# Loading transformed data four steps ahead, and copying turned weight pieces with the scalar engine

## The chip, the cores and the metric

The kernel runs on one core of one Trainium2 chip. The metric is the device time of one execution in microseconds (us); lower is better. TensorE is written PE, its weight loads PEld, VectorE DVE, ScalarE ACT, GpSimd POOL. SyncE (SP) computes nothing here: it issues nearly all transfers, in the order of the program, and where a transfer has to wait for a buffer or for data, SP stands still and everything behind it waits too.

## The reference, cut to what matters

```python
X = np.fft.rfft(x, axis=1)                      # x: 8 batches x 3072 x 256
Yr = Xr @ w_r - Xi @ w_i + b_r                  # mixing, complex, 256 x 256
Yi = Xr @ w_i + Xi @ w_r + b_i
Y  = shrink(Yr) + 1j * shrink(Yi)               # towards zero by 0.01
y  = np.fft.irfft(Y, n=3072, axis=1)            # 24576 tokens x 256
h  = y @ w_in;  g = h - tanh(h);  x2 = g @ w_out          # d_ff = 2048
logits = x2 @ phi                               # 32 slots
# soft mixture of 8 experts: softmax over tokens in, softmax over slots out
```

All is float32 at the interface.

## The kernel before

The kernel has three parts: a spectral phase (the transform, the mixing and the way back, to about 700 us), a token phase (the gate and the logits, chunk by chunk) and a short expert phase. The change touches the spectral phase alone.

**The spectral phase** does a real transform of length 3072 as 96 x 32. For each batch, `f1_half` multiplies by the 96-point table and stores the result to DRAM (`ad`), in 8 pieces. `load_a2` reads it back in another order: one transfer of 512 KB holds the data of two *pairs* of frequency groups. `f2_pair` does the 32-point transform of one pair. `split_sum`, `mix_part`, `add_bias` and `shrink` do the mixing, `i1_pair` the first stage of the way back, `i2_half` the second.

The loop at L576 runs over steps `s`: step `s` does `f2_pair` of pair `i` of batch `b`, with `b, i = divmod(s, 12)`, so there are 96 steps of some 6 to 9 us, and in the same step the mixing of pair `s-1`, `i1_pair` of pair `s-2`, the way back of an earlier batch, and the first stage of a later batch (`piece`). An even step issues `load_a2` for step `s + 2`. Its tiles come from the pool `fa2`, which has three buffers. Nothing is scheduled by the compiler here: each engine runs the instructions in the order in which the program writes them.

**The pieces of weights.** `w_out` and `w_in` come as 64-bit floats, in 32 pieces, four for each batch of 12 steps. In a step `s` that has a piece, `load_w` loads it into the one buffer `raw`; `narrow`, one step later, queues 11 DVE instructions that make float32 values out of it, which `pump` hands out over two steps (L505, L508). `use_w` at `s+4` turns the piece on PE into the PSUM tile `pt` (L453) and DVE copies `pt` to `wt` (L455). `fold_w` at `s+5` multiplies it (`pw`); for the 16 pieces of `w_out` DVE writes the negative to `wp` (L488), for the 16 of `w_in` DVE adds it up in `mw` (L478, L480).

**The bank.** `pf2` of `f2_pair`, `pt` and `pw` share one PSUM tag, `f2`, with a single buffer. So `f2_pair` of a step can start only when its data `a` has landed and when the last `pt` or `pw` of the step before has been read out.

On SP the order within a step is: stores of the step before (`flush`), loads of `x`, loads `v2`, stores and loads of the weight pieces, stores of `y`, `load_a2`, and last `load_w`.

Of the kernel before, what the change touches and what calls it, by code (L numbers as in the profile page):

```python
# [12 lines left out]
AF = mybir.ActivationFunctionType  # L13
ALU = mybir.AluOpType
# [110 lines left out]
def spectral_phase(tc, nb, x, w_r, w_i, b_r, b_i, tb, yd, w_in, w_out, phi, ident, wo32, md, wh, wl, wp, wy, ew):  # L125

    nc = tc.nc
    with ExitStack() as late, ExitStack() as mid, ExitStack() as ctx:
# [32 lines left out]
        NP = NG // 2  # L161
# [20 lines left out]
        def load_f2(g0, g1):  # L182
            nc.sync.dma_start(out=f2[:, 128 * g0:128 * g1], in_=tb["f2"][:, 128 * g0:128 * g1])
# [16 lines left out]
        def load_mix():  # L200
            for w in (w_r, w_i):
                t = thp.tile([128, 512], F32, tag="sw", name="wst", bufs=3)
                nc.sync.dma_start(
                    out=t.rearrange("p (h e) -> p h e", h=2), in_=w.rearrange("(h p) e -> p h e", p=128)
                )
                tables.append(t)
# [10 lines left out]
        def load_tables():  # L217
            nc.sync.dma_start(out=i1, in_=tb["i1"])
            nc.sync.dma_start(out=bias[:, 0:256], in_=b_r.partition_broadcast(128))
            nc.sync.dma_start(out=bias[:, 256:512], in_=b_i.partition_broadcast(128))  # L220
            nc.gpsimd.memset(dh.bitcast(F32), 0.0)
            nc.gpsimd.memset(dl_.bitcast(F32), 0.0)
# [214 lines left out]
        def use_w(j):  # L437
            src, r, q = pieces[j]
            t = wnew.pop(j)
            if src is w_in:  # L440
                n = slice(256 * (q % 2), 256 * (q % 2) + 256)
                if wl[r][q // 2] is None:
                    wl[r][q // 2] = ew.wp.tile([128, 512], F32R, tag=f"wl{r}{q // 2}", name="wl")
                h = wh[r][q // 2][:, n]
                nc.scalar.activation(h, t, AF.Copy)
                nc.gpsimd.tensor_tensor(
                    out=wl[r][q // 2][:, n], in0=t, in1=h.bitcast(F32), op=ALU.subtract
                )
            else:
                nc.sync.dma_start(out=wo32[128 * r:128 * r + 128], in_=t)  # L450
            pt = ps.tile([128, 2, 128], F32, tag="f2", name="pt", bufs=1)
            for k in range(2):
                nc.tensor.transpose(pt[:, k, :], t[:, 128 * k:128 * k + 128], ident)  # L453
            wt = dcp.tile([128, 2, 128], F32, tag="wt", name="wt")
            nc.vector.tensor_copy(wt, pt)  # L455
            wtr[j] = wt

        def load_wf(j):
# [7 lines left out]
        def fold_w(j):  # L466

            src, r, q = pieces[j]
            wt = wtr.pop(j)
            if src is w_in:  # L470
                pw = ps.tile([128, 288], F32, tag="f2", name="pw", bufs=1)
                wf = wfs.pop(j)
                for k in range(2):
                    F = 2 * q + k
                    nc.tensor.matmul(pw[:, 0:256], wt[:, k, :], wf[:, k], start=k == 0, stop=k == 1, skip_group_check=True)
                    nc.tensor.matmul(pw[:, 256:288], wt[:, k, :], wp[:, F, :], start=False, stop=k == 1, skip_group_check=True)
                if q == 0:
                    nc.vector.tensor_scalar(out=mw, in0=pw, scalar1=-1.0, scalar2=None, op0=ALU.mult)  # L478
                else:
                    nc.vector.tensor_tensor(out=mw, in0=mw, in1=pw, op=ALU.subtract)  # L480
                if q == 7:
                    nc.sync.dma_start(out=md[128 * r:128 * r + 128], in_=mw[:, 0:256])
                    nc.vector.tensor_copy(wy[:, r], mw[:, 256:288])
                return
            pw = ps.tile([128, 32], F32, tag="f2", name="pw", bufs=1)
            for k in range(2):
                nc.tensor.matmul(pw, wt[:, k, :], ph[:, k, :], start=k == 0, stop=k == 1)
            nc.vector.tensor_scalar(out=wp[:, r, :], in0=pw, scalar1=-1.0, scalar2=None, op0=ALU.mult)  # L488

        chores = []  # L490

# [34 lines left out]
        if True:  # L526
            load_f2(0, 2)
            for i in range(8):
                for j in range(2):
                    f1_half(0, i, j)  # L530
                if i == 2:
                    load_mix()
            split_mix()
            load_a2(0, 0)
            load_f2(2, 8)
            load_tables()
            load_f2(8, 16)
            load_f2(16, NG)
            load_late_tables()
            T = nb * NP  # L540

            pieces_at = {}
            for k in range(1, nb):
                for j in range(8):
                    pieces_at[NP * (k - 1) + j + (2 if k == 1 else 0)] = (k, j)

            def piece(t):
                return [pieces_at[t]] if t in pieces_at else []

            for t in range(3):  # L550
                for j in piece(t):
                    load_x(*j)

            i2_at, v2_at, y_steps = {}, {}, {}
            for k in range(nb):
                t = NP * k + NP
                if k < nb - 2:
                    steps = [t + 4 + j for j in range(4)] + [t + 8 + j // 2 for j in range(8)] + [t + 12 + j for j in range(4)]
                    gap = 1
                else:  # L560
                    steps = [t + 4 + j // 2 for j in range(16)]
                    gap = 1
                for j in range(8):
                    for u in range(2):
                        i2_at.setdefault(steps[2 * j + u], []).append((k, j, u))
                    v2_at.setdefault(max(t + 3, steps[2 * j] - 3), []).append((k, j))
                for h in range(2):
                    for u in range(3):
                        t1 = steps[8 * h + 7] + 1 + gap * u
                        y_steps.setdefault(t1 if k < nb - 1 else T + NP - 1, []).append((k, h, 2 * u))  # L570

            slots = [NP * k + j for k in range(nb) for j in range(1, 9, 2)]
            due_w = {}
            for j in range(len(pieces)):
                due_w.setdefault(slots[len(slots) * j // len(pieces)], []).append(j)
            for s in range(T + NP):  # L576
                b, i = divmod(s, NP)
                flush()
                if s < T:
                    f2_pair(b, i)  # L580
                pump(1)
                for j in due_w.get(s - 1, ()):
                    narrow(j)
                for j in piece(s + 3):
                    load_x(*j)
                m = divmod(s - 1, NP) if 1 <= s <= T else None
                if m:
                    mix_part(*m, 0)
                    add_bias(*m)
                for j in v2_at.get(s, ()):  # L590
                    load_v2(*j)
                for j in piece(s):
                    f1_half(*j, 0)
                due = i2_at.get(s, ())
                for j in due[:(len(due) + 1) // 2]:
                    i2_half(*j)
                for j in due_w.get(s - 5, ()):
                    fold_w(j)
                for j in due_w.get(s - 4, ()):
                    use_w(j)  # L600
                for j in due_w.get(s - 3, ()):
                    load_wf(j)
                if s < T:
                    split_sum(b, i)
                pump(3)
                if m:
                    mix_part(*m, 1)
                if m:
                    mix_part(*m, 2)
                for j in piece(s):  # L610
                    f1_half(*j, 1)
                if m:
                    shrink(*m)
                pump(2)
                for j in due[(len(due) + 1) // 2:]:
                    i2_half(*j)
                if 2 <= s <= T + 1:
                    i1_pair(*divmod(s - 2, NP))
                for j in y_steps.get(s, ()):
                    store_y(*j)  # L620
                if 4 <= s < 12:
                    load_i2(s - 4)
                if s + 2 < T:
                    load_a2(*divmod(s + 2, NP))
                for j in due_w.get(s, ()):
                    load_w(j)
                if s == T:
                    ctx.close()
                if s == T + 3:
                    mid.close()  # L630
                yield
# [865 lines left out]
```

## Time and profile before

| | |
|---|---|
| time, median of 3 runs | 2306.78 us (2300.38 to 2307.19) |
| time of the profiled execution | 2304.85 us |
| its span, first to last instruction | 2302.7 us |
| mean granted clock of PE | 0.989 |
| PE busy | 2224.2 us, 97% of the span |
| DVE busy | 1761.4 us, 76% |
| ACT busy | 1449.5 us, 63% |
| POOL busy | 656.4 us, 29% |
| transfers, share of the 16 DMA engines on SP's queue | 76.7% |

An engine's row says how long it had an instruction in work. PE is in work nearly all the time, so the time is PE's work plus what PE stands still, plus what it loses where the granted clock is 0.5 instead of 1.0 (1.2 in place of 2.4 GHz).

### The profile page before, as it was taken

What the parts mean: (1) busy time and instruction counts of PE and PEld (TensorE: products, weight loads), DVE (VectorE), ACT (ScalarE), POOL (GpSimd) and SP (SyncE); (2) the same over time, 40 slices, a digit from 0 to 9 for tenths busy, and PEclk for the clock granted to TensorE, in tenths of its full rate; (3) what the DMA queues carried; (4) which work ended last, traced back from release to release, by engine and by line L of the source; (5) the groups of instructions that cost most, each with busy time, mean ns of one, the idle gap of its engine ahead of it and who ended that gap; (6) DMA issues with size and microseconds to landing.
All of it is one profiled execution on the core that took longest, in us unless ns stands there. A gap on an engine that the chain in (4) does not pass through costs nothing.

```text
span 2302.7 us, 51129 instructions
## 1 busy us (share of the span) xinstructions
PE 2224.2 (97%) x19832; PEld 1823.4 (79%) x19832; DVE 1761.4 (76%) x3605; ACT 1449.5 (63%) x2347; POOL 656.4 (29%) x666
## 2 busy tenths in 40 slices
PE   6899999999989999999999999999999999999989
PEld 4677777878878888888888888888887888888757
DVE  4888787888885877778777877777877787777634
ACT  2455565556545777667667676767767677666624
POOL 1333333434432422222222222222222222222111
PEclk8999999999999999999999999999999999999999
DMA  8678888888666777777777777777777777777899
GB/s 231 215 210 255 245 248 240 248 251 250 206 212 193 169 179 186 177 171 174 168 176 178 176 180 184 182 175 175 172 169 175 175 180 179 186 174 175 238 342 366
DMA packets 404018, 471.16 MB, mean 205 GB/s; under 512 B 36160, under 2 KB 351808, under 8 KB 403392
## 3 DMA queue, kind: packets, MB, share of 16 engines
q1 hardware_dynamic: 403664, 467.85, 76.7%
q8 instruction: 157, 2.57, 0.5%
q14 instruction: 85, 0.70, 0.1%
q10 hardware_dynamic: 112, 0.04, 0.0%
HBM read 164.45 MB, written 106.17 MB: 118 GB/s over the span
## 4 chain that ended last, share of the span: by engine, by line
PE 56%; DMA 6%; SPq 3%; ACT 1%; issue 0%; DVE 0%; ACTq 0%
PE ph L771 35%; PE pd L1020 7%; PE pl L892 6%; DMA yr<-yd 4%; PE p_out L1319 3%; SPq L860 3%; PE pd L812 2%; DMA ewt<-in_moe_w 2%; PE pl L828 1%; PE pl L900 1%; ACT g L782 0%; DMA gq<-in_moe_w 0%; SPq L1006 0%; DVE gt L846 0%; SPq L1308 0%
## 5 line engine op out<-in xcount | busy, mean ns | idle before, releaser
L782 ACT ACTIVATE g<-ph 128x512 f32<-128x512 f32 x752 | 448.4, 596 | 378.2 <-PE ph L771 353.4
L789 DVE TENSOR_TENSOR g<-ph,g 128x512 f32<-128x512 f32 x564 | 373.3, 676 | 157.1 <-PE ph L771 146.8
L846 DVE STREAM_TRANSPOSE gt<-g 128x512 f32<-128x512 f32 x752 | 476.1, 681 | 12.9 <-DMA gq<-gt 7.8
L771 PE MATMUL ph<-th,s 128*128 128x256 f32 x2256 | 482.0, 286 | 2.1 <-ACT g L782 2.1
L771 PEld LDWEIGHTS ph<-th,s 128*128 128x128 f32 x2256 | 377.8, 189 | 41.4 <-issue 19.4
L793 ACT ACTIVATE g<-g 128x1024 f32<-128x1024 f32 x376 | 392.6, 1054 | 1.5
L771 PE MATMUL ph<-tl,s 128*128 128x256 f32 x1128 | 318.3, 282 | 0.0
L771 PE MATMUL ph<-y,wh 128*128 128x256 f32 x1128 | 316.4, 280 | 0.0
L771 PE MATMUL ph<-yh,wl 128*128 128x256 f32 x1128 | 315.7, 280 | 0.0
L771 PE MATMUL ph<-yh,wh 128*128 128x256 f32 x1128 | 315.6, 280 | 0.0
L684 POOL TENSOR_TENSOR tl<-tr,th 128x512 fp32r<-128x512 f32 x94 | 122.1, 1300 | 383.1 <-ACT th L683 349.6
L678 POOL TENSOR_TENSOR tr<-y 128x256 f32<-128x256 f32 x92 | 68.1, 740 | 553.8 <-DMA y<-yd 553.8
L372 POOL TENSOR_TENSOR sw<-t,c 64x256 f32<-64x256 f32 x192 | 169.5, 883 | 182.2 <-DVE c L364 155.2
L771 PEld LDWEIGHTS ph<-tl,s 128*128 128x128 f32 x1128 | 213.8, 190 | 0.0
L771 PEld LDWEIGHTS ph<-yh,wh 128*128 128x128 f32 x1128 | 212.9, 189 | 0.1
L771 PEld LDWEIGHTS ph<-yh,wl 128*128 128x128 f32 x1128 | 212.4, 188 | 0.0
L771 PEld LDWEIGHTS ph<-y,wh 128*128 128x128 f32 x1128 | 212.2, 188 | 0.1
L892 PE MATMUL pl<-g,wp 128*32 128x256 f32 x3072 | 196.8, 386 | 0.0
L1020 PE MATMUL pd<-gq,et 128*32 128x512 f32 x1504 | 181.6, 593 | 0.5 <-DMA gq<-gt 0.5
L281 PEld LDWEIGHTS pf<-f,a 128*128 128x128 f32 x768 | 102.1, 198 | 94.3 <-issue 34.0
L407 PEld LDWEIGHTS pi<-i,v 96*128 96x128 f32 x1024 | 130.2, 195 | 26.1 <-issue 19.9
L281 PE MATMUL pf<-f,a 128*128 128x128 f32 x768 | 108.0, 286 | 42.8 <-DMA a<-ad 22.0
(225 smaller groups left out, 4586.3 us busy)
## 6 DMA issues: line engine op xcount, KB each, us to landing
gq<-gt SPq DMA_DIRECT2D x1504, 128.0 KB, 3.1
xt<-in_x SPq DMA_DIRECT2D x64, 384.0 KB, 5.8
vd<-vs SPq DMA_DIRECT2D x96, 256.0 KB, 4.1
v<-vd SPq DMA_DIRECT2D x64, 384.0 KB, 6.5
yd<-yt SPq DMA_DIRECT2D x48, 512.0 KB, 5.9
y<-yd SPq DMA_DIRECT2D x48, 512.0 KB, 5.9
yr<-yd SPq DMA_DIRECT2D x48, 512.0 KB, 4.1
a<-ad SPq DMA_DIRECT2D x47, 512.0 KB, 6.5
```

The source lines that it names most:

```text
L281: nc.tensor.matmul(p[:, :, h, gg, :], t[:, gg, 128 * h:128 * h + 128], f2[:, 128 * g:128 * g + 128], start=True, stop=True,)
L372: eng.tensor_tensor(out=v[64 * ri:64 * ri + 64, gg], in0=t[q, e], in1=c[q, e], op=ALU.subtract)
L407: nc.tensor.matmul(p[:, a, :], t[:, 4 * u + a, :], i2[:, 96 * n2:96 * n2 + 128], start=True, stop=True)
L684: nc.gpsimd.tensor_tensor(out=lo, in0=t, in1=hi.bitcast(F32), op=ALU.subtract)
L771: nc.tensor.matmul(o[:, 256 * j:256 * j + 256], a[u][:, 128 * j:128 * j + 128], y[v], start=new and j == 0 and k == 0, stop=n in (2, 3, 4) ...
L782: nc.scalar.activation(e[n], o.rearrange("p (j n) -> p j n", j=2), AF.Copy)
L789: nc.vector.tensor_tensor(out=h, in0=o, in1=h, op=ALU.add)
L793: nc.scalar.activation(g, g, AF.Tanh)
L846: nc.vector.transpose(out=t[:, :, 2 * (p % 4) + u, :], in_=g[:, u, :].rearrange("p (c i) -> p c i", i=32))
L860: nc.sync.dma_start(out=o[32 * q:32 * q + 32], in_=t[32 * a:32 * a + 32, q])
L892: nc.tensor.matmul(lp[c][q:q + 32, 0:256], wp[:, 2 * p + f, :], half_of(gs[c, p + f // 2][:, f % 2], h), start=p == 0 and f < 2, stop=Fals ...
L1020: nc.tensor.matmul(o[32 * a:32 * a + 32, f], ex[c][:, k, :], g[a][:, k], start=k == 0, stop=k == 3)
```

## The change

Loads of `a` are issued two steps earlier, that is four steps ahead of their use. The second load of the first batch moves to the start, directly behind the second part of the table `f2`. The first pair of the second batch (t = 12) keeps its place two steps ahead, and t = 14 goes directly behind it. The first pairs of the batches after that (t = 24, 36, ..., 84) are loaded four steps ahead as well, which is the step whose `flush` issues the last store of that batch's `ad`. The three buffers stay. The copy of `pt` to `wt` and the negation of `pw` into `wp` go from DVE to ACT; `mw` stays on DVE.

```diff
@@ use_w
             wt = dcp.tile([128, 2, 128], F32, tag="wt", name="wt")
-            nc.vector.tensor_copy(wt, pt)
+            nc.scalar.activation(wt, pt, AF.Copy)
             wtr[j] = wt
@@ fold_w
-            nc.vector.tensor_scalar(out=wp[:, r, :], in0=pw, scalar1=-1.0, scalar2=None, op0=ALU.mult)
+            nc.scalar.activation(wp[:, r, :], pw, AF.Copy, scale=-1.0)
@@ before the loop
             load_a2(0, 0)
             load_f2(2, 8)
+            load_a2(0, 2)
             load_tables()
@@ end of step s
-                if s + 2 < T:
-                    load_a2(*divmod(s + 2, NP))
+
+                for t in (s + 2, s + 4):
+                    if 4 <= t < T and (t == NP) == (t == s + 2):
+                        load_a2(*divmod(t, NP))
                 for j in due_w.get(s, ()):
                     load_w(j)
```

(`load_a2` does nothing for odd pairs; `NP` is 12 and `T` is 96.)

## Rows read from the trace of the kernel before

**Rows 1.** Groups of instructions; busy us, mean ns, idle us before it with releasers.

```profile
L281 PE MATMUL pf<-f,a 128*128 128x128 f32 x768 | 108.0, 286 | 42.8 <-DMA a<-ad 22.0 <-DVE wt L455 9.0 <-DVE t L363 3.7
```

**Rows 2.** Busy time by stretch: PE, PEld, DVE, ACT, POOL, clock, DMA share, GB/s.

```profile
60.00:192.00 132.00, 121.91 (x752) 93.34 (x751) 117.02 (x248) 67.36 (x118) 49.41 (x60) 0.99 0.76 225
192.00:700.00 508.00, 486.17 (x3242) 404.08 (x3240) 429.45 (x876) 292.19 (x486) 195.98 (x233) 0.98 0.79 235
```

**Rows 3.** Timeline around step 46, SP: start us, duration us, instruction.

```profile
336.20 0.38 SPq L153 DMA_DIRECT2D ad<-asb  x1
...
338.20 1.02 SPq L269 DMA_DIRECT2D a<-ad  x1
```

**Rows 4.** Timeline of PE at the start of step 46.

```profile
347.40 1.17 PE L281 MATMUL pf<-f,a 128*128 128x128 f32 x8 [3.52 <-DVE c L364]
```

**Rows 5.** Tile a, 337 to 349 us: its transfers.

```profile
DMA to landing us min/median/max: 7.8/8.4/9.1
```

**Rows 6.** Waits of SP, 60 to 700 us: total us, times, longest.

```profile
SPq L431 <- DVE dl L508: 150.1, 24, 8.2
...
SPq L269 <- DMA ad<-asb: 1.0, 1, 1.0
```

**Rows 7.** Timeline of the first steps, all engines.

```profile
28.72 2.05 PE L281 MATMUL pf<-f,a 128*128 128x128 f32 x8 [6.90 <-DMA a<-ad]
...
33.27 0.57 SPq L269 DMA_DIRECT2D a<-ad  x1
...
34.75 0.35 SPq L431 DMA_DIRECT2D raw<-in_moe_w_out  x1
...
44.81 2.05 PE L281 MATMUL pf<-f,a 128*128 128x128 f32 x8 [6.66 <-DMA a<-ad]
...
49.99 0.28 DVE L505 TENSOR_SCALAR da<-raw 128x256 int32<-128x256 int32 x1
```

**Rows 8.** Tile raw, 34 to 36 us: its transfer.

```profile
DMA to landing us min/median/max: 12.7/12.7/12.7
```

**Rows 9.** Busy time by stretch, first steps; columns as in rows 2.

```profile
38.00:44.80 6.80, 0.14 (x2) 0.02 (x1) 2.38 (x4) 0.00 (x0) 1.75 (x2) 0.73 1.07 228
```

**Rows 10.** Waits of PE, 60 to 192 us.

```profile
PE pf L281 <- DVE wt L455: 6.4, 5, 1.6
PE pf L281 <- DMA a<-ad: 1.5, 2, 0.9
PE pf L281 <- DVE wp L488: 1.2, 1, 1.2
PE pi L379 <- POOL sw L372: 0.6, 1, 0.6
```

**Rows 11.** Waits of DVE, 50 to 192 us.

```profile
DVE da L505 <- DMA raw<-in_moe_w_out: 7.7, 6, 1.5
DVE xml L293 <- ACT xmh L292: 2.7, 3, 1.3
```

**Rows 12.** Groups of instructions by shape; columns as in rows 1.

```profile
L455 DVE COPY wt<-pt 128x256 f32<-128x256 f32 x32 | 13.2, 412 | 0.0
...
L920 ACT ACTIVATE le<-pl 64x256 f32<-64x256 f32 x47 | 17.3, 367 | 0.0
```

**Rows 13.** Line L488: duration ns min/median/max, first and last start us.

```profile
L488 DVE TENSOR_SCALAR wp<-pw x16: 179/181/193, 77.9 to 366.2; 128x32 f32<-128x32 f32 x16
```

**Rows 14.** Busy time by stretch, around three waits; columns as in rows 2.

```profile
263.00:270.00 7.00, 7.00 (x36) 7.00 (x35) 4.17 (x9) 2.27 (x4) 1.68 (x3) 0.51 0.65 237
...
348.00:352.00 4.00, 4.00 (x24) 4.00 (x23) 3.59 (x6) 1.63 (x3) 1.25 (x2) 0.57 1.03 361
...
652.00:659.00 7.00, 4.33 (x20) 4.36 (x21) 6.04 (x13) 2.66 (x5) 2.49 (x3) 0.51 0.46 142
```

**Rows 15.** Waits of ACT, 60 to 700 us.

```profile
ACT xmh L311 <- DVE xmf L304: 74.2, 49, 4.0
```

**Rows 16.** Page, part 6: issues, KB each, median us to landing.

```profile
ad<-asb SPq DMA_DIRECT2D x58, 384.0 KB, 4.0
```

## The prediction

> **What bounds the kernel now.** I read the page first: PE is in work for 97% of the span and the chain that ended last runs mostly through PE, so time is won only where PE stands still or runs at the low clock. Then I read the groups by shape for the line where the change acts. Before the first product of `f2_pair` PE stood idle for 42.8 us in all [rows 1]; that is the whole pool from which this change can draw directly. Then the busy time by stretch, for who stands behind PE: DVE is in work for 117.0 of 132 us from 60 to 192 us, and for 429.5 of 508 us from 192 to 700 [rows 2]. ACT has 292.2 of 508 there, so it has room.
>
> The names that the list of waits gives need a check, since `f2_pair` waits for two things at once: its data and the bank. Step 46 shows how. PE stood idle 3.52 us until 347.40, put down to DVE L364 [rows 4], which `f2_pair` does not need. SP issued the load for this step at 338.20 [rows 3], and the longer of the two transfers in that stretch took 9.1 us [rows 5]: it landed at 347.3, and PE started 0.1 us later. This was a wait for the load. Why was it issued so late? `load_w` waits for the single buffer `raw`, until DVE has done the last of the 11 instructions on the piece before: SP stood there 150.1 us in all, 24 times, up to 8.2 us [rows 6]. Everything behind `load_w` is held, also the next step's load of `a`, which is needed two steps later at most.
>
> So there are two independent causes, in part at the same steps: loads that come late because SP stands, and a bank that DVE empties late because it is behind with its queue. Taking one away alone would leave the other. The change takes both.
>
> **The change part by part.** I split the 42.8 us by time. *Start:* 6.90 us before the very first `f2_pair`, whose load is not moved, and 6.66 us for the second load [rows 7], which is. *60 to 192 us:* 6.4 + 1.5 + 1.2 = 9.1 us [rows 10]. *After 192 us:* the rest, 42.8 - 6.9 - 6.7 - 9.1 = 20.1 us, of which I count 19, leaving 1 for waits of other kinds.
>
> *Start.* The second load was issued at 33.27 and PE waited for it until 44.81 [rows 7]. From 38 to 44.8 us the DMA engines were full, share 1.07 at 228 GB/s [rows 9]. Placed behind `f2[2:8]` it goes ahead of the other tables and the first pieces of `x`, so it should be there when PE asks at 38.1; the 6.66 us vanish for PE. But the load of t = 4 now takes its old place, which is ahead of the first `raw`. That transfer was issued at 34.75 and took 12.7 us [rows 8], so it landed at 47.4. With 512 KB more ahead of it at 228 GB/s it lands 2.2 us later, an estimate of 49.7. DVE first touched `raw` at 49.99 [rows 7], and `shrink` stands behind that in DVE's queue. So DVE gets on only 0.3 us earlier (2.5 us if `raw` isn't delayed), while PE gets on 6.7 us earlier and then waits for `shrink`.
>
> *60 to 192 us.* Here PE cannot pass DVE. DVE's idle time from 50 to 192 us is mostly 7.7 us of waiting for `raw` and 2.7 us of waiting for ACT's `xmh` [rows 11]; the first is made by its own queue (end of one piece, load, first instruction of the next) and stays. And PE already waited for the output of `shrink` at `i1_pair` [rows 10], so a wait removed from `f2_pair` reappears there. What the stretch gains is what DVE gains: 0.3 us from the start, eight copies `wt` at 0.41 us [rows 12] = 3.3 us, of the eight `wp` at 0.18 us [rows 13] those two that are not just ahead of a wait for `raw` = 0.4 us, and the 2.7 us in which DVE waited for work. That is 6.7 us at most, of 15.8 us that vanish at `f2_pair`. I take 5.5.
>
> *After 192 us.* Here DVE has time to catch up in every batch: it is idle for 78.5 of 508 us [rows 2], and only four of twelve steps' pieces overload it. So a wait that vanishes is mostly won. Also DVE loses 0.41 us of work in every second step with pieces. I take 16 of the 19 us; the other 3 go where DVE, now behind a faster PE, brings the sums or `shrink` too late.
>
> *Clock.* Three times after 192 us the granted clock stood at 0.51 to 0.57 for 4 to 7 us [rows 14], each time behind one of the longest waits at `f2_pair`. PE was in work for 7.0, 4.0 and 4.33 us of these. At the full level, 2.4 instead of 1.2 GHz, that work takes half: 3.5 + 1.7 + 2.2 = 7.4 us at most. Without the long waits I expect the clock to stay up, and take 5.5.
>
> *ACT.* It gets 32 copies of 128x256 out of PSUM. No such shape is there; the nearest is the copy of 64x256 out of PSUM at 367 ns [rows 12]. With 16 small ones at, say, half of that: 32 x 0.37 + 16 x 0.18 = 14.7 us, 3% of ACT's time up to 700 us. They stand in ACT's queue ahead of the copy in `split_sum`, where ACT waited 74.2 us in 49 times for DVE [rows 15]; that wait hides them. Bounds: nothing, or all 14.7 us if that cover were gone.
>
> *SP.* The number of transfers doesn't change. The loads of t = 24, 36, ... 84 come in the step in which their last `ad` is stored, and SP must wait for the landing. That is a rival, below. The token phase isn't touched; what PE wins before it, the end wins.
>
> The sum: 5.5 + 16 + 5.5 = 27 us. Against the profiled execution (2304.85 us, 2.2 us of it outside the span) that is 2277.9; it lies 1.9 us under the median of the runs shown. I predict 2278 us.
>
> **The rivals.**
>
> 1. *DVE is the bound everywhere.* Then waits at `f2_pair` turn into waits at `i1_pair` and at the mixing in all batches, and only DVE's own relief counts: 0.3 + 32 x 0.41 + some 0.7 of the `wp` = 14 us at most, 9 if a third of that only lengthens waits for `raw`. For it speaks DVE at 89% of 60 to 192 us, against it the 78.5 us of idle time after that. Time 2291 to 2296.
>
> 2. *SP stands at the batch borders.* In step 44 the last store of `ad` was issued at 336.20 and the load of that step at 338.20 [rows 3]; a store of `ad` lands after 4.0 us [rows 16]. With t = 48 in that place SP stands for 4.0 - 2.0 = 2 us more, at six borders 12 us, and with it the stores and loads `v2` behind it. If all of that reached PE, 27 - 12 = 15 us would be left: 2290. It decides only if the stores behind it then come later than two buffers allow; their sources are used again two steps, some 13 us, later. The Trainium skill (DMA: Bandwidth & Descriptors, "Two DMAs through the same engine are not ordered") states the rule against this placing: a transfer that reads what an earlier one writes must be held back at the issuing engine until the earlier one is complete, being behind it in the same queue is not enough. By that rule the trace agrees: SP stood 1.0 us at a load of `a` for a store of `ad`, once [rows 6].
>
> 3. *All is won, the start too.* If `raw` isn't delayed and DVE doesn't hold PE: 15.8 + 19 + 7.4 = 42 us, 2263.
>
> 4. *The other side: ACT becomes late.* If the copies `wt` delayed `xmh`, and through it DVE and the mixing, every one of the 48 would cost its duration, 14.7 us, and what is won at the bank would be lost behind it: slower by up to 14.7 us, 2320. It decides from the point where ACT no longer waits for DVE at `split_sum` [rows 15].
>
> 5. *Nothing moves*, because another late transfer (the pieces of `x`, `v2`) takes the place of `a`: 2305.
>
> **How the numbers follow.** This kernel's measurement can tell about 0.3%, 7 us, from no change. Chances: the forecast (24 to 34 us won, 2271 to 2281) 0.53; DVE the bound 0.24; SP at the borders 0.07; all won 0.07; nothing 0.05; ACT late 0.04. The first four are faster by over 0.3%; I keep 0.01 of them for ends near the limit. So faster 0.90, same 0.06, slower 0.04. The range reaches up to the end of the first rival and of the second and, below, half way to the third: 2268 to 2296.
>
> **What would show it.** In the profile after: idle time before `f2_pair` down from 42.8 us to about 7 to 12 us, with the first 6.9 us still there and neither `a` nor `wt` named; PE waiting at `i1_pair` for `sw`, and DVE for `raw` for some 6 us, in the first four steps; new waits of PE for POOL `sw`, `xmh` or `t` of 5 to 10 us below 192 us; no stretch at the low clock between 60 and 700 us; ACT's wait at `split_sum` shorter by about the copies. A mixing that waits as long as `f2_pair` did before, in the later batches too, would make the prediction wrong, and so would a clock that falls without such waits.

## The result, and the profile after

The changed kernel takes 2288.93 us in the median of four runs (2288.32 to 2291.63), beside 2306.99 us for the kernel before on the same chip. The ratio is 0.9919, with a 95% interval from 0.9889 to 0.9948: about 19 us faster, 12 to 26. The forecast was 2278, that is 29 us under the median shown; the time lies in the range of 2268 to 2296. So the sign was right, and the gain came out at two thirds of what was forecast. It lies 8 us above the forecast's own bracket (2271 to 2281) and 2 us under that of rival 1 (2291 to 2296): the range held because it reached to the end of that rival, and part of what rival 1 says is what happened, as shown below. The profiled execution took 2291.63 us with a span of 2289.8 us, and the mean granted clock of PE rose from 0.989 to 0.996.

The groups by shape, in the columns of [rows 1], show the line on which the change acts:

```profile
L281 PE MATMUL pf<-f,a 128*128 128x128 f32 x768 | 104.1, 279 | 13.4 <-DMA a<-ad 8.0 <-DVE mw L480 3.2 <-DMA f<-tab_f 2.2
```

The idle time before `f2_pair` fell from 42.8 to 13.4 us, and `wt` is gone from its causes. Of the 8.0 us for `a`, 7.4 is the very first load, which was not moved. That is 29 us of idle time gone, but the token phase starts only 16.4 us earlier. The list of PE's waits (in all, times, longest; rows of other lines left out) says where the rest stands now:

```profile
PE pa L322 <- DVE t L352: 9.0, 15, 1.0
PE pf L281 <- DMA a<-ad: 8.0, 2, 7.4
...
PE pi L379 <- POOL sw L372: 3.7, 5, 1.4
PE pf L281 <- DVE mw L480: 3.2, 8, 0.5
...
PE pf L281 <- DMA f<-tab_f: 2.2, 1, 2.2
```

The first product of the mixing now waits until DVE's `add_bias` (L352) has read its bank, and `f2_pair` until DVE has read `pw` into `mw`. Neither was a large wait before.

Busy time by stretch, in the columns of [rows 2], cut at the starts of steps 24 and 95:

```profile
60.00:187.00 127.00, 119.20 (x729) 91.23 (x729) 112.75 (x228) 67.73 (x131) 47.46 (x57) 1.00 0.77 233
187.00:674.00 487.00, 475.35 (x3183) 392.58 (x3181) 420.38 (x825) 287.37 (x510) 191.28 (x229) 1.00 0.81 243
```

The clock is 1.00 in both; the low stretches of [rows 14] are gone, as are the long waits that the prediction put before them. DVE's share did not fall: 89% of the first stretch, as before, and 86% of the second after 85%. DVE has lost the copies, but PE now asks for everything sooner.

To place the gain I compare when PE starts `f2_pair` of the same step in the two profiled executions (start in us, from the timeline of PE):

| step | before | after | gained so far |
|---|---|---|---|
| 2 | 44.81 | 38.24 | 6.6 |
| 12 | 112.36 | 108.36 | 4.0 |
| 24 | 191.76 | 187.11 | 4.7 |
| 48 | 361.08 | 347.76 | 13.3 |
| 95 | 690.91 | 674.15 | 16.8 |
| first product of the token phase | 702.7 | 686.3 | 16.4 |
| end | 2302.7 | 2289.8 | 12.9 |

Of 16.8 us, 8.6 come from steps 24 to 48, whose pieces are of `w_out`, and only 3.5 from the twice as long stretch from 48 to 95, whose pieces are of `w_in`. In the token phase the profiled pair lose 3.5 us again. I take that as scatter: PE waited there 9.1 us for `yr` before and 12.0 us after, and in the runs below these waits lie between 11.2 and 23.8 us, and the phase takes between 1602.4 and 1620.7 us (1600.0 before, 1603.5 after), without order by the edit. So I judge the spectral phase by the start of step 95, and whole times by the ratio to the kernel before on the same chip. The start of step 95 scatters too: two kernels below were profiled twice, and it came at 674.15 and 673.82 us in the one, at 652.51 and 657.60 in the other. Differences under some 5 us there tell nothing.

**The steps one by one.** At the start, the timeline of PE shows the second product of `f2_pair` (start, duration, instruction, idle time before it and its cause):

```profile
33.28 2.05 PE L281 MATMUL pf<-f,a 128*128 128x128 f32 x8 [2.22 <-DMA f<-tab_f]
```

and that of DVE its first touch of `raw`:

```profile
42.49 0.68 DVE L352 TENSOR_TENSOR t<-pa,bias 128x512 f32<-128x512 f32 x1
47.78 0.29 DVE L505 TENSOR_SCALAR da<-raw 128x256 int32<-128x256 int32 x1 [4.61 <-DMA raw<-in_moe_w_out]
```

Step 2 no longer waits for its load, and DVE gets to `raw` 2.2 us sooner than in [rows 7] (49.99), not 0.3. But it does stand 4.61 us for it, with `shrink` behind it, and of 6.6 us won by PE 4.0 are left at step 12.

On SP the list of waits from 60 to 700 us has, beside others:

```profile
SPq L431 <- DVE dl L508: 141.9, 23, 9.3
...
SPq L269 <- DMA ad<-asb: 10.0, 6, 3.5
```

The first is the wait at `load_w` of [rows 6], hardly shorter: the loads of `a` still stand behind it, but with four steps of lead they are there in time. The second is rival 2's wait: 10.0 us at six borders, where 12 were worked out.

On ACT the two copies (groups by shape, 60 to 700 us) cost 16.7 us in all:

```profile
L455 ACT ACTIVATE wt<-pt 128x256 f32<-128x256 f32 x32 | 13.0, 405 | 0.3 <-PE pt L453 0.3
L488 ACT ACTIVATE wp<-pw 128x32 f32<-128x32 f32 x16 | 3.7, 232 | 0.1
```

### The profile page after: what moved, and what is told of

The parts are those of the page before. It is cut to its first block, busy times and chain, and to the rows that moved or that the text cites. A ratio compares the mean times of both kernels' runs of the same rounds, so it can differ in the third digit from the quotient of the medians.

```text
span 2289.8 us, 51156 instructions
## 1 busy us (share of the span) xinstructions
PE 2221.4 (97%) x19832; PEld 1816.7 (79%) x19832; DVE 1759.3 (77%) x3557; ACT 1451.2 (63%) x2395; POOL 655.9 (29%) x666
## 4 chain that ended last, share of the span: by engine, by line
PE 58%; DMA 7%; SPq 2%; ACT 1%; issue 0%; DVE 0%; ACTq 0%
PE ph L774 36%; PE pd L1023 7%; PE pl L895 6%; DMA yr<-yd 4%; PE p_out L1322 3%; PE pd L815 2%; DMA ewt<-in_moe_w 2%; SPq L863 1%; PE pl L831 1%; PE pl L903 1%; ACT g L785 1%; DMA gq<-wo 0%; SPq L1009 0%; DMA gq<-in_moe_w 0%; DVE gt L849 0%
## 5 line engine op out<-in xcount | busy, mean ns | idle before, releaser
L849 DVE STREAM_TRANSPOSE gt<-g 128x512 f32<-128x512 f32 x752 | 476.0, 680 | 13.4 <-DMA gq<-gt 8.2
L672 POOL TENSOR_TENSOR y<-y,yh 128x1024 fp32r<-128x1024 f32 x46 | 110.5, 2402 | 124.9 <-issue 124.8
```

Source lines behind the costliest of these rows:

```text
L672: eng.tensor_tensor(out=t, in0=yl.pop(c).bitcast(F32), in1=hi.bitcast(F32), op=ALU.subtract)
L849: nc.vector.transpose(out=t[:, :, 2 * (p % 4) + u, :], in_=g[:, u, :].rearrange("p (c i) -> p c i", i=32))
```

## The experiments

The main theory, A in what was written ahead of the runs: the two causes cover each other, and what is left below 700 us is DVE with its loop over the single buffer `raw` (load, 11 instructions, next load), which holds SP as well. Its rivals stand in each expectation with what they say.

**One part at a time.** First the new loads alone (`wt` and `wp` back on DVE):

```diff
-            nc.scalar.activation(wt, pt, AF.Copy)
+            nc.vector.tensor_copy(wt, pt)
...
-            nc.scalar.activation(wp[:, r, :], pw, AF.Copy, scale=-1.0)
+            nc.vector.tensor_scalar(out=wp[:, r, :], in0=pw, scalar1=-1.0, scalar2=None, op0=ALU.mult)
```

> The loads as in the changed kernel, the copies wt and wp back on DVE. Theory A (two independent causes, late loads and a bank that DVE empties late): the bank's part stays, idle time before f2_pair between 20 and 28 us with wt named first, time 2293 to 2301, that is 6 to 14 us under the kernel before. Theory B (the loads do it all): idle time before f2_pair near the 13.4 us of the changed kernel, time 2287 to 2292.

Then the copies on ACT alone, with the loads where they were:

```diff
-            load_a2(0, 2)
...
-                for t in (s + 2, s + 4):
-                    if 4 <= t < T and (t == NP) == (t == s + 2):
-                        load_a2(*divmod(t, NP))
+                if s + 2 < T:
+                    load_a2(*divmod(s + 2, NP))
```

> The copies wt and wp on ACT, the loads as in the kernel before. Theory A: the loads still come late, idle time before f2_pair 28 to 36 us with the load of a named, low clock still behind the longest ones, time 2297 to 2305. Theory B (the loads do it all): no difference from the kernel before. Rival C (the copies alone free DVE and with it SP, so that the loads come early enough too): idle time before f2_pair under 20 us, time 2287 to 2293.

The same group as above, first of the loads alone:

```profile
L281 PE MATMUL pf<-f,a 128*128 128x128 f32 x768 | 107.1, 284 | 31.1 <-DVE wt L455 20.3 <-DMA a<-ad 6.7 <-DMA f<-tab_f 1.5
```

and of the copies alone:

```profile
L281 PE MATMUL pf<-f,a 128*128 128x128 f32 x768 | 107.9, 286 | 38.0 <-DMA a<-ad 35.4 <-ACT asb L252 1.3 <-ACT xmf L290 0.7
```

The loads alone gave 0.9952 (0.9932 to 0.9973), the copies alone 0.9994 (0.9975 to 1.0012), both together 0.9919. The idle time fell by 11.7 us with the loads, by 4.8 with the copies, by 29.4 with both, so either one leaves most of what the other would take. Read the names: with the copies gone from DVE, the wait named `wt` vanishes and 35.4 us are put down to `a`, which was 22.0 before; with the loads early, `a` shrinks to the unmoved first load and `wt` has 20.3, which was 9.0. Each cause stood behind the other, as the prediction read it. Step 95 starts 9.0 us earlier with the one, 2.4 with the other (inside the scatter), 16.8 with both. Both idle times are above what I had expected (20 to 28 and 28 to 36 us), so more was hidden than I thought. The time of the copies alone came out as theory B has it, no different from before; that the loads do it all is excluded by the loads alone, which leave 31.1 us where B had some 13.4.

**What is left: the loop over `raw`.** On the changed kernel, a second buffer:

```diff
-            raw = dcp.tile([128, 256, 2], I32, tag="raw", name="raw", bufs=1)
+            raw = dcp.tile([128, 256, 2], I32, tag="raw", name="raw", bufs=2)
```

> The changed kernel with two buffers for raw. Theory A (what is left is DVE's throughput, in which its own loop through raw counts): DVE's waits for raw, 32 us from 50 to 700 us, nearly vanish, SP no longer stands at load_w, and the spectral phase ends 8 to 20 us earlier: 2269 to 2281. Rival D (PE's own work bounds what is left, or DVE merely waits elsewhere): within 3 us of the changed kernel, 2286 to 2292.

And DVE nearly free of the pieces, one instruction of the 11 left:

```diff
-            scalar(a, hi, 3, ALU.logical_shift_left, 0x7FFFFFFF, ALU.bitwise_and)
-            scalar(li, hi, -0x80000000, ALU.bitwise_and, 0x40000000, ALU.bitwise_xor)
-            tensor(a, a, li, ALU.bitwise_xor)
-            scalar(lo, lo, 8, ALU.logical_shift_right)
             scalar(l, lo, 2.0 ** -44, ALU.mult)
-            scalar(lo, a, -0x800000, ALU.bitwise_and)
...
-            tensor(l, l, lof, ALU.mult)
```

> The changed kernel in which narrow does one of its 11 DVE instructions, so that the pieces of w_out and w_in are not computed: 10 x 0.45 us of DVE work less for each of 32 pieces, 144 us. Theory A: with DVE light PE waits nowhere for sums, shrink or mw; PE's idle time from 60 to 700 us falls from some 25 us to under 8 and the time to 2255 to 2272. Rival D (PE's own work bounds what is left): no more than 4 us under the changed kernel, 2285 to 2290.

With two buffers the time is 2277.24 us, 0.9861 (0.9840 to 0.9882), and step 95 starts at 656.8, another 17.4 us before the changed kernel. SP's largest wait at `load_w` (3.2 us with four smaller ones), and DVE's at `raw`, in the lists of waits (SP 60 to 690, DVE 50 to 690 us):

```profile
SPq L431 <- DVE dl L505: 2.2, 5, 1.4
```

```profile
DVE da L505 <- DMA raw<-in_moe_w_in: 1.7, 2, 1.0
DVE da L505 <- DMA raw<-in_moe_w_out: 0.3, 1, 0.3
```

In the changed kernel the same two were 141.9 us on SP and, from 50 us on, 16.9 + 15.4 us on DVE. DVE does no instruction less; it only no longer stands still between pieces.

With one instruction per piece (0.9801, 0.9782 to 0.9820) the windows, cut at the same steps, show PE at work for all but 1.85 of 581 us:

```profile
60.00:173.00 113.00, 112.50 (x727) 89.61 (x726) 81.07 (x154) 68.95 (x128) 47.41 (x57) 1.00 0.85 247
173.00:641.00 468.00, 466.65 (x3184) 391.24 (x3183) 317.63 (x587) 293.24 (x510) 188.76 (x230) 1.00 0.85 253
```

So nearly all that the changed kernel still loses between 60 us and step 95 it loses to DVE's work on the pieces: step 95 starts 33 us earlier when DVE is light, and half of that is bought by one buffer, with all of DVE's work in place.

**Why the loads had come late.** The copies on ACT and two buffers `raw`, but the loads as before (the two diffs above together):

> Two buffers for raw and the copies on ACT, but the loads of a two steps ahead and in the place of the kernel before. Theory A (loads came late because SP stood at load_w for DVE): with SP free they land in time, waits for a after step 4 under 4 us, and apart from the 6.6 us at the start the spectral phase is as fast as with two buffers and early loads; time 2277 to 2288. Rival H (two steps ahead is too short by itself, the transfers being slow): waits for a of 12 us or more after step 4, time 2288 or more.

Group, and the wait of SP at `load_w` for the pieces from 60 to 690 us (5.9 us with its waits there for other DVE instructions):

```profile
L281 PE MATMUL pf<-f,a 128*128 128x128 f32 x768 | 104.5, 280 | 16.5 <-DMA a<-ad 14.5 <-DVE mw L480 1.3 <-ACT xmf L290 0.7
```

```profile
SPq L431 <- DVE dl L505: 2.0, 4, 1.4
```

All 14.5 us for `a` lie in two waits before 52 us; after that no step waits for its load, though it is issued only two steps ahead. So two steps are lead enough; the loads came late because SP stood at `load_w`, and the alternative, that the lead itself was too short, falls. The time is 0.9897 (0.9873 to 0.9921). Step 95 starts at 661.2, 4.4 us behind the run with two buffers and early loads. That is no more than the scatter, and 4.35 of it are there at step 24: with two buffers, issuing earlier may be worth something at the start, and nothing after it. No run gave the second buffer to the kernel before by itself, without the copies on ACT.

**The start.** The first load of `raw` goes directly behind the second load of `a`:

```diff
             load_a2(0, 2)
+            load_w(0)
             load_tables()
...
-                    load_w(j)
+                    if j:
+                        load_w(j)
```

> The changed kernel with the first load of raw at the start, directly behind the second load of a. Theory A (at the start DVE stands 4.6 us for raw, and up to step 11 DVE sets the pace): that wait goes, step 12 starts 2 to 4.5 us earlier than in the changed kernel, and little of it lasts to the end of the spectral phase where later batches are paced by DVE too: 0 to 4 us in the time. Rival E (PE's own work sets the pace of the first steps): step 12 within 1 us of the changed kernel.

DVE's wait for `raw` at the start fell from 4.61 to 1.3 us, yet step 12 began no earlier, at 109.04 us (108.36 and 109.80 in two runs of the changed kernel). The list of PE's waits from 28 to 66 us has one that was 1.4 us in the changed kernel:

```profile
PE pf L248 <- DMA xt<-in_x: 4.3, 1, 4.3
```

A piece of `x` has taken the place of `raw`. My theory for the start, that DVE's wait for `raw` holds it, is wrong: one transfer is exchanged for another. Rival E, PE's own work, does not follow: in the run with one instruction per piece step 12 starts at 97.82, 10.5 us before the changed kernel, so DVE's work counts there too. The time, 0.9945 (0.9930 to 0.9960), tells nothing more.

**The borders.** The loads of the first pair of every batch two steps ahead, so that SP has no landing to wait for:

```diff
-                    if 4 <= t < T and (t == NP) == (t == s + 2):
+                    if 4 <= t < T and (t % NP == 0) == (t == s + 2):
```

> The changed kernel with the loads of t = 24, 36, ... 84 two steps ahead, as that of t = 12. Theory A: SP's 10 us of waits for stores of ad go, and nothing else: the time within 2 us of the changed kernel, since what stands behind them has slack. Rival F (SP standing at the borders takes back part of the gain): 3 to 10 us faster than the changed kernel.

It gave 0.9956 (0.9940 to 0.9971), which decides nothing without the changed kernel on the same chip. So both ran once more side by side:

> The changed kernel once more, as the measure for the kernels that run beside it. Where the load yr lands late in the token phase, times of all kernels differ between chips by some 5 us, the ratio to the kernel before should come out again within its interval, 0.989 to 0.995; step 95 starts between 673 and 677 us.

> The loads at the batch borders two steps ahead, now beside the changed kernel on one chip. Theory A (SP's waits there cost nothing): step 95 starts within 2 us of the changed kernel and the times agree within 3 us. Rival F' (two steps ahead is too late at the borders again, as the first run of it could be read): 6 us or more slower than the changed kernel, with waits for a before f2_pair of the border steps.

The changed kernel gave 0.9933 (0.9911 to 0.9956), the other 0.9937 (0.9913 to 0.9960): no difference. SP's wait at L269 from 60 to 690 us, in the changed kernel:

```profile
SPq L269 <- DMA ad<-asb: 9.9, 6, 3.5
```

and with the borders two steps ahead:

```profile
SPq L269 <- DMA ad<-asb: 1.4, 1, 1.4
```

Step 95 starts at 673.82 with the wait and at 674.75 without. The 10 us on SP are real and cost PE nothing that these runs can tell. (The changed kernel's ratio here, 0.9933, and in the result, 0.9919, lie inside each other's intervals.)

**A version faster than both kernels.** Two buffers `raw`, two of DVE's scratch, and the last float32 product, sum and product of each piece on POOL:

```diff
-            raw = dcp.tile([128, 256, 2], I32, tag="raw", name="raw", bufs=1)
+            raw = dcp.tile([128, 256, 2], I32, tag="raw", name="raw", bufs=2)
...
-            a = dcp.tile([128, 256], I32, tag="a", name="da")
+            a = dcp.tile([128, 256], I32, tag="a", name="da", bufs=2)
...
-            tensor(l, l, lof, ALU.mult)
-            tensor(l, l, af, ALU.add)
...
-            scalar(lof, hi, float(897 << 20), ALU.is_ge)
-            tensor(l, l, lof, ALU.mult)
+            scalar(hi.bitcast(F32), hi, float(897 << 20), ALU.is_ge)
+            for k, f in ((lof, ALU.mult), (af, ALU.add), (hi.bitcast(F32), ALU.mult)):
+                chores.append((lambda k=k, f=f: nc.gpsimd.tensor_tensor(out=l, in0=l, in1=k, op=f),))
```

> The changed kernel with two buffers for raw and for a piece's scratch tile, and the three float32 products and sums of narrow on POOL: 3 x 0.45 us less on DVE for each piece, 43 us in all. Theory A (DVE's throughput is what is left): 4 to 12 us faster than with two buffers alone, that is 2266 to 2274. Rival G (POOL's half of shrink and of the sum comes late behind the new work, 3 x 0.75 us per piece): no faster than with two buffers alone, 2276 to 2290.

> The fastest version so far once more, beside the changed kernel: 12 to 20 us under it.

It gave 0.9855 (0.9830 to 0.9880) and, beside the changed kernel, 0.9858 (0.9832 to 0.9884): 2280.11 us where the changed kernel had 2297.36. That is no more than two buffers alone (0.9861): the three instructions taken from DVE buy nothing that this can tell. It is the outcome of rival G, but not by its cause: PE's waits for POOL from 60 to 690 us are 2.0 and 2.1 us in the two runs, beside 2.1 with two buffers alone, and its listed waits for DVE fell from 4.4 to 1.7 and 2.3. All three small edits at once (two buffers, first `raw` early, borders two steps ahead) came out the same:

> The changed kernel with two buffers for raw, the first load of raw at the start, and the loads at the batch borders two steps ahead. Theory A: the start's wait counts more where the later stretches are paced less by DVE: 1 to 6 us under two buffers alone, 2271 to 2276.

0.9860 (0.9845 to 0.9874), where I had expected 1 to 6 us under two buffers alone. Step 95 starts at 652.82, 4.0 us earlier than with these, inside the scatter. Of the three edits only the second buffer shows an effect.

## Why the prediction was right, and where it was off

**Right: two causes behind one line, and who sets them.** That the loads are late because SP stands at `load_w`, that the bank is emptied late because DVE is behind, and that taking one leaves the other: shown by the idle times of the two single parts and by the run with two buffers and the old loads.

**Start and first stretch: 5.5 forecast, 4.7 measured at step 24.** The size held, the path to it only in part. PE's wait of 6.66 us vanished and part of it came back through `raw`, as worked out. But `raw` landed at 47.8, not 49.7. And the exchange of `raw` for `x` shows that `raw` is not the only limit there. Of the signs named, DVE's wait for `raw` came at 4.6 us where some 6 were forecast, PE's at `i1_pair` for `sw` at 1.4 us in the first four steps (3.7 in the whole run); 2.2 us for the second part of the table `f2` were not foreseen.

**After 192 us: the step that was mis-sized.** The prediction says "Here DVE has time to catch up in every batch", and so that "a wait that vanishes is mostly won", 16 of 19 us. By stretches it was this:

| steps | waits that vanished at `f2_pair` | new waits in PE's list | gained, measured | of it clock, as below |
|---|---|---|---|---|
| 24 to 48 | 6.8 us | 0.8 us | 8.6 us | 1.6 us |
| 48 to 95 | 12.2 us | 8.9 us (L352 5.7, of which 0.4 were there before, `mw` 3.2) | 3.5 us | 0.0 us |

Without the clock 7.0 + 3.5 = 10.5 us were won. From 24 to 48 the step held: 7.0 for 6.8. From 48 to 95 it failed: 3.5 of 12.2. (The second trace of the changed kernel gives 3.4 us at step 24 and 8.2 and 5.5 us for the two stretches: the same picture, with each number good to some 2 us.) There the waits turned into waits for DVE, which is rival 1: right for most of this stretch, and wrong for the one before it. The sign that the prediction named against itself, a mixing that waits as long as `f2_pair` did, came by nearly half: 5.7 us for 12.2. The idle 78.5 us of [rows 2] were the wrong evidence: a sum over a stretch does not say that DVE is idle when PE needs it. Step 58, in the timeline, shows it:

```profile
417.03 0.68 DVE L352 TENSOR_TENSOR t<-pa,bias 128x512 f32<-128x512 f32 x1
...
417.86 0.36 PE L322 MATMUL pa<-wah,xmh 128*128 128x256 f32 x1 [0.89 <-DVE t L352]
```

DVE is there in work from 405 to 424.6 us but for one wait of 1.19 us for `raw`, so `add_bias` reads its bank late and PE stands. In the next step the `mw` that stayed on DVE holds the bank of `f2_pair`:

```profile
424.78 0.94 PE L281 MATMUL pf<-f,a 128*128 128x128 f32 x6 [0.45 <-DVE mw L480]
```

That DVE's pieces cause these waits is shown: PE stands for 1.85 us in 581 without them. Why the stretch with `w_in` lost more than the one with `w_out` is only argued: there DVE keeps a read of the bank, 0.44 us of `mw`, in place of the `wp` that went to ACT. No run moved `mw`.

**Clock: 5.5 forecast, some 1.6 gained.** It stayed up, as forecast. I measure what that gave by the two steps behind each long wait. Windows from the start of one step to that of the second after it, in the columns of [rows 2], first steps 34 and 35, then 46 and 47, before:

```profile
261.80:277.04 15.24, 15.24 (x94) 14.28 (x95) 10.26 (x25) 6.89 (x11) 5.00 (x6) 0.78 0.66 200
347.40:361.08 13.68, 13.68 (x95) 12.72 (x96) 10.04 (x25) 6.94 (x11) 5.00 (x6) 0.88 0.69 210
```

and after:

```profile
254.01:267.69 13.68, 12.99 (x95) 11.34 (x94) 13.00 (x30) 8.04 (x16) 5.11 (x7) 1.00 0.95 290
334.08:347.76 13.68, 12.97 (x96) 11.32 (x94) 13.00 (x30) 8.08 (x16) 5.12 (x7) 1.00 1.00 312
```

The clock is back at 1.00, but only the first pair of steps got shorter, by 1.6 us; the second takes 13.68 us both times, and steps 90 and 91 take 15.00 in place of 14.97 (13.69, 13.69 and 14.99 in the second trace of the changed kernel). By the mean clocks of these windows (0.78, 0.88, and 0.86 for steps 90 and 91) the low clock had cost some 3.4 + 1.6 + 2.1 = 7.1 us before, an estimate from one minus the clock times the length. In the first step of each pair 2.3, 0.8 and 0.2 us came back, and 0.8, 0.8 and 0.2 were lost again in the second. In steps 35 and 47 PE stands for the sums, which follow DVE's L304, in waits too short for its list; step 47 shows them at the weight loads:

```profile
342.24 0.19 PEld L322 LDWEIGHTS pa<-wah,xmh 128*128 128x128 f32 x1 [0.31 <-ACT xmh L311]
...
342.89 0.19 PEld L322 LDWEIGHTS pa<-wah,xml 128*128 128x128 f32 x1 [0.36 <-POOL xml L312]
```

So the clock's term failed as the waits' did: what it gave back went largely into waits behind DVE. How much is put down to the clock and how much to the waits depends on where the steps are cut; the total does not.

**ACT.** Hidden, as forecast, at 16.7 us in place of 14.7 (405 ns each where the nearest row gave 367, 232 where half of it gave 184). That ACT's wait at `split_sum` would get shorter was wrong: it grew from 74.2 to 119.7 us, which fits a DVE that PE has caught up with. That excludes rival 4, which needed this wait gone.

**SP.** Rival 2's wait came at the size worked out (10.0 for 12 us) and cost nothing that the runs can tell.

**The sum.** 4.7 + 10.5 + 1.6 = 16.8 us at step 95, where 5.5 + 16 + 5.5 = 27 were forecast. Of the 10.2 us between them 5.5 are the waits after 192 us, all of it from step 48 on, and 3.9 the clock; behind both stands DVE, which the prediction had idle enough.

## What to carry to other kernels

When one instruction waits for two things, sum its idle time over both, and ask for each what would remain if the other were taken away: alone they were worth 0.5% and nothing, together 0.8%. Before a load is moved earlier, look for what holds its queue: here SP stood 150 us at the reload of one scratch buffer, and on top of the change a second buffer won another 17.4 us at the end of the phase, as much as the change itself (16.8), with not one instruction less. The idle time of an engine over a stretch is no room for a faster neighbour; look in the timeline whether it is idle in the steps where the waits are.

## What the runs showed of the hardware that was not expected

A load that stood ahead in the queue landed later, in most runs, with another directly behind it. The transfer `f2[2:8]` landed 4.4 us after its issue before; with the second load of `a` issued 0.50 us behind it, the row of that tile says, for the changed kernel:

```profile
DMA to landing us min/median/max: 6.1/6.1/6.1
```

In the eleven runs with that load behind it the landing took 4.4 to 6.1 us, in the three without it 4.3 to 4.4. In the changed kernel PE waited 2.2 us for it at step 1, where it had waited 0.7 us for ACT before, so part of the 6.66 us taken away at step 2 came back one step earlier.

The landing of `yr` in the token phase, which no edit touches, goes with a phase that differs by some 20 us between runs (1600.0 to 1620.7; waits of PE for it 9.1 to 23.8 us). That is as large as the effect under study, and a start time ahead of that phase tells edits apart, down to some 5 us, where the whole time does not.
